# Four pieces per low half on GpSimd, rank preparations one step earlier, and the second weights fetched from SyncE

## The chip, the cores and the metric

The kernel runs on one core of a Trainium2 chip. The time is that of the whole program on the device in microseconds; three executions are given by their median. In this text PE is TensorE, DVE is VectorE, ACT is ScalarE, POOL is GpSimd and SP is SyncE, which here only issues DMAs.

## The reference, cut to what matters

Three layers follow each other. Attention over 4 batches, 8 heads, 576 positions and a head size of 64, with a window of 32 in heads 0 to 3 and a dilated window in heads 4 to 7. Then a mixture of 8 experts in which each of the 2304 tokens goes to the one expert with the largest gate value. Then a dense layer with a rational activation.

```python
logits = x @ w_gate + modality_bias[modality_id]        # x: [2304, 512] from the attention
e_idx = np.argmax(logits, axis=1)
for e in range(8):
    mask = e_idx == e
    h = np.maximum(x[mask] @ w1[e], 0.0)                # w1[e]: [512, 1024]
    out[mask] = gate_w[mask, None] * (h @ w2[e])        # w2[e]: [1024, 512]
# then: h = x @ w_in; g = P(h) / (Q(h) + 1e-6); g @ w_out
```

## The kernel before, in words

Every product is done in float32 by halves: a float32 matrix is split into a high half (an ACT copy to the matmul's number format) and a low half (the rest, one subtraction), and three matmuls, high by high, high by low and low by high, are summed in PSUM.

The attention is a pipeline of 36 steps, `for g in range(NG)`. In each step PE makes the scores of four blocks (`step_s`, line 485), DVE adds the mask and finds the maximum (line 489), ACT takes exponentials (`step_e`, line 496), PE transposes them (`step_t`, line 503), DVE copies the transposes (line 505), PE multiplies by the values (`step_v`, line 515) and DVE divides (lines 520 to 529). PE also transposes q and k for later steps (`qk_T`, lines 463 and 469) and works through `tasks`, a list of the gate's transposes and matmuls (lines 549, 562, 567). Engines run their instructions in the order in which the program writes them, so the order in a step is the order on each engine.

The first half of the tokens (`bp` 0) is finished in the middle of this loop. From then on `soon`, a list built by `ahead`, adds one small piece of work to each step: counting, choosing the expert with the most tokens (`choose`), fetching its first weights (`fetch`), building one-hot rows (`spread`, line 318), then `take`, which finds that expert's first 256 tokens and gathers them through two indirect DMAs of POOL (line 365), then `order` (lines 371 to 379), which prepares ranks for the other experts, and at last a reduction of what `order` left on POOL (line 303). `take` runs at the end of step 33, `order` at the end of step 34, the reduction at the end of step 35.

When the last q and k are transposed, at the end of step 33, their load buffers are given up (`lctx.close()`), and the split first weights (`w1s`) and the raw second weights (`raw2`) get that memory. In steps 34 and 35 and right after the loop ACT and POOL split the first expert's first weights, `raw1`, in eight chunks of 128 x 512: ACT copies the high half (line 130), POOL subtracts the low half (line 131). After the loop ACT reads the chosen expert's number, and it issues the two 1 MB loads of `raw2` (`fetch2`, line 213).

After the loop PE ends the attention while it starts the first slot of 128 tokens of the chosen expert: `stage_1` (lines 146, 148, 150) with the first weights, then the second half of the gate (lines 562 to 579, `pick` on DVE, lines 283 to 289), the ranks of the second half (lines 850, 851, 295, 297), a chain of small DVE instructions that ends in the table of token places (lines 865 to 892), and PE's product with that table (line 907). Between these, PE does the slot's second matmuls (`mm2_first`: lines 803 and 805 for chunks 0 to 7, then line 809). ACT and POOL split the second weights in eight chunks meanwhile (`hi2`, line 784; `lo2`, line 788). The four matmuls of chunks 0 and 1 and the four of chunks 2 and 3 stand ahead of line 907 on PE, those of chunks 4 to 7 behind it. The first pieces of `stage_1` for the second slot stand ahead of line 907 too.

The remaining slots follow, with weights swapped where the expert changes, and then the dense layer.

SP issues nearly all DMAs in program order. `put_x` writes finished attention rows to DRAM: 20 DMAs for the third quarter (lines 602 and 605, written at step 29), two for the last (line 593, written after the loop).

Of the kernel before, what the change touches and what calls it, by code (L numbers as in the profile page):

```python
# [85 lines left out]
PL = 1  # L86
NSLOT = 25
NC2 = NSLOT + 8
TINY = 32
# [39 lines left out]
def split(nc, src, hi, lo, kk, eng):  # L129
    nc.scalar.activation(out=hi[:, kk], in_=src[:, kk], func=AF.Copy)  # L130
    eng.tensor_tensor(out=lo[:, kk], in0=src[:, kk], in1=hi[:, kk].bitcast(F32), op=ALU.subtract)


# [33 lines left out]
def fused(ctx, tc, io):  # L167
# [155 lines left out]
    def ahead(ps):  # L323
# [46 lines left out]
        def order():  # L370
            low = C("lower").rearrange("p (a b) -> p a b", a=8)
            V.tensor_scalar(out=nfo, in0=fo, scalar1=-1.0, scalar2=1.0, op0=ALU.mult, op1=ALU.add)
            V.scalar_tensor_tensor(out=nfe[:, 0, :], in0=C("slot")[:, 0:8], scalar=1.0, in1=nfo[:, 0, :], op0=ALU.add, op1=ALU.mult)
            V.tensor_scalar(out=o16, in0=nfe, scalar1=KEY, scalar2=None, op0=ALU.mult)
            V.tensor_tensor(out=LB, in0=low, in1=fo.to_broadcast([128, 8, 8]), op=ALU.max)
            nc.gpsimd.tensor_tensor(out=LB, in0=LB, in1=nfo.rearrange("p o e -> p e o").to_broadcast([128, 8, 8]), op=ALU.mult)
            V.scalar_tensor_tensor(out=c16[:, 0, :], in0=fo[:, 0, :], scalar=256.0, in1=c0, op0=ALU.mult, op1=ALU.max)
            V.scalar_tensor_tensor(out=R0[:, 0:HT], in0=nfe.to_broadcast(N9), scalar=KEY, in1=R0[:, 0:HT], op0=ALU.mult, op1=ALU.add)
            own.append(own_rank(R0, 0, nc.gpsimd))

        return [[], [count], [choose, fetch, place], [place2], *[[lambda i=i, j=j: spread(i, j)] for i in range(2) for j in range(2)], [take], [order], [lambda: own.pop()()]]

    with ExitStack() as actx, tc.manual_schedule(), nc.allow_low_precision(reason="integers"):
# [249 lines left out]
        nsp = 0  # L633
        done_V = 2
        for g in range(NG):
            if g < NG:
# [18 lines left out]
            if w1s:  # L655
                for _ in range(2):
                    if nsp < 8:
                        n, kk = divmod(nsp, 4)
                        split(nc, raw1[n], w1s[0][n], w1s[1][n], kk, nc.gpsimd)
                        nsp += 1  # L660
            if 0 <= g - LAG1 < NG - 1:
# [11 lines left out]
            if done_T == 4 * NU and not w1s:  # L673
# [3 lines left out]
                wr2 = w2ctx.enter_context(tc.tile_pool(name="wraw2", bufs=1, side="right", reuse_waits="tile"))  # L677
                raw2.extend(wr2.tile([128, 4, 512], F32, name=f"raw2{n}") for n in range(2))
            if done_L < NC and done_T >= 8 * (done_L - 1):
                load(done_L)  # L680
                done_L += 1
# [4 lines left out]

        def split1(n):
            nonlocal nsp
            for i in range(nsp, nsp + n):
                split(nc, raw1[i // 4], w1s[0][i // 4], w1s[1][i // 4], i % 4, nc.gpsimd)  # L690
            nsp += n

        e = nc.scalar.value_load(ft[0:1, 0:1], min_val=0, max_val=7)
        for n in range(2):
            fetch2(n, e, nc.scalar)
        step_e(NG - 1)
# [30 lines left out]
def moe(ctx, tc, io, sh):  # L727
# [57 lines left out]

    def lo2(c, eng):
        n, kk = divmod(c, 4)
        eng.tensor_tensor(out=w2l[n][:, kk], in0=raw2[n][:, kk], in1=w2h[n][:, kk].bitcast(F32), op=ALU.subtract)

# [40 lines left out]
    sh["spread"](0, 0)  # L830
    lo2(0, nc.gpsimd)
    fill(slot0, 2)
    tasks.pop(0)()
    for c in range(1, 8):
        if c == HC:
            fill(slot0, F1)
        hi2(c)
        lo2(c, nc.vector if c in () else nc.gpsimd)
    sh["spread"](0, 1)
# [792 lines left out]
```

## Time and profile before

| what | value |
|---|---|
| median of three executions | 826.1 us (820.74 to 828.68) |
| profiled execution, its own time | 826.8 us |
| its span, first to last instruction | 825.0 us |
| granted TensorE clock, mean | 0.979 |
| PE busy | 791.3 us, 96% of the span |
| DVE busy | 577.6 us |
| ACT busy | 509.7 us |
| POOL busy | 149.0 us |
| chain that ended last | PE 83%, DMA 8%, DVE 4%, ACT 3% |

Times inside the profile count from the first instruction. The own time of the profiled execution is 1.8 us longer than its span. A granted clock of 1.00 is the higher level of TensorE's clock (2.4 GHz), 0.50 the lower (1.2 GHz). The chain is found by going back from the last instruction, at each step to what released it.

### The profile page before, as it was taken

To read this page: it belongs to the slowest core of one execution; us is meant where nothing else is said; L and a number is where in the kernel's file an instruction comes from. 1 tells how busy PE (TensorE), PEld (TensorE's weight loads), DVE (VectorE), ACT (ScalarE), POOL (GpSimd) and SP (SyncE) were. 2 spreads that over 40 slices of the span, in tenths; PEclk is the share of its full clock that TensorE was granted. 3 is DMA by queue.
4 is the path that set the end of the run, shared out by engine and by line. 5 is a ranking of instruction groups with operands and counts; after the bars stand their busy time and mean duration, and the time that the engine had idled before them with its cause. 6 is when DMAs were issued, how large, how long until landed. Compare 5 with 4: busy or idle time off the path is not lost.

```text
span 825.0 us, 15207 instructions
## 1 busy us (share of the span) xinstructions
PE 791.3 (96%) x5277; PEld 638.4 (77%) x5279; DVE 577.6 (70%) x1370; ACT 509.7 (62%) x993; POOL 149.0 (18%) x191
## 2 busy tenths in 40 slices
PE   7899997899998999999989999999999999999995
PEld 4777765687786678888768888888888888999894
DVE  3776788932252224895599987887788888888894
ACT  4655666234253325663689878777687678778783
POOL 2011008421110101231174512000020002001001
PEclk9998899999999999999999999999999999999998
DMA  7968947195947686774011001200020001001001
GB/s 189 160 145 150 191 147 199 51 339 211 333 153 288 247 306 209 236 276 158 18 39 39 14 1 38 66 1 1 0 69 22 1 0 65 1 1 38 1 1 38
DMA packets 73509, 91.58 MB, mean 111 GB/s; under 512 B 33577, under 2 KB 43323, under 8 KB 73403
## 3 DMA queue, kind: packets, MB, share of 16 engines
q1 hardware_dynamic: 68531, 76.38, 32.7%
q0 software_dynamic: 3360, 11.03, 3.8%
q10 hardware_dynamic: 1512, 2.91, 1.1%
q8 instruction: 48, 0.79, 0.4%
q14 instruction: 58, 0.48, 0.2%
HBM read 75.59 MB, written 14.71 MB: 109 GB/s over the span
## 4 chain that ended last, share of the span: by engine, by line
PE 83%; DMA 8%; DVE 4%; ACT 3%; issue 1%; SPq 0%; POOL 0%; POOLq 0%; ACTq 0%; DVEq 0%
PE p1t L1363 8%; PE p1t L1364 8%; PE p1t L1365 8%; DMA sw<-in_w 5%; PE p1t L146 4%; PE p1t L150 4%; PE p1t L148 4%; PE pht L1533 4%; PE pht L1534 3%; PE pht L1535 3%; PE pot L777 3%; PE pot L775 3%; PE pot L779 3%; PE pot L1535 2%; PE pxt L1533 2%; PE pxt L1534 2%
## 5 line engine op out<-in xcount | busy, mean ns | idle before, releaser
L1481 ACT ACTIVATE raw<-p1t 128x512 f32<-128x512 f32 (+1 forms) x78 | 43.2, 554 | 81.9 <-PE p1t L1365 77.0
L1488 DVE TENSOR_TENSOR raw<-raw,raw 128x512 f32<-128x512 f32 (+1 forms) x80 | 52.0, 649 | 59.0 <-ACT raw L1482 58.2
L768 DVE TENSOR_TENSOR hl<-pht,hh 128x512 fp32r<-128x512 f32 x34 | 21.9, 685 | 97.9 <-ACT hh L767 92.7
L1365 PE MATMUL p1t<-yh,wl 128*128 128x512 f32 (+1 forms) x240 | 89.0, 371 | 0.0
L1544 POOL DMA_INDIRECT out<-hs,row x10 | 10.9, 1087 | 302.2 <-ACT hs L1542 300.8
L1482 ACT ACTIVATE raw<-raw,bab 128x512 f32<-128x512 f32 (+1 forms) x80 | 61.9, 773 | 2.7
L1363 PE MATMUL p1t<-yh,wh 128*128 128x512 f32 (+1 forms) x160 | 59.6, 372 | 0.3 <-DVE m L1499 0.3
L1364 PE MATMUL p1t<-yl,wh 128*128 128x512 f32 (+1 forms) x160 | 59.2, 370 | 0.0
L1510 DVE SCALAR_TENSOR_TENSOR m<-m,nab,raw 128x512 f32<-128x512 f32 (+1 forms) x80 | 58.6, 733 | 0.1
L146 PE MATMUL p1t<-w1h,xh 128*128 128x512 f32 x144 | 57.7, 401 | 0.1
L150 PE MATMUL p1t<-w1h,xl 128*128 128x512 f32 x144 | 56.7, 393 | 0.0
L148 PE MATMUL p1t<-w1l,xh 128*128 128x512 f32 x144 | 56.4, 392 | 0.0
L1508 DVE SCALAR_TENSOR_TENSOR raw<-raw,raw 128x512 f32<-128x512 f32 (+1 forms) x80 | 56.4, 705 | 0.0
L1483 ACT ACTIVATE raw<-p1t,nab 128x512 f32<-128x512 f32 (+1 forms) x78 | 56.1, 719 | 0.0
L1490 ACT ACTIVATE raw<-raw,bab 128x512 f32<-128x512 f32 (+1 forms) x80 | 53.7, 671 | 0.5 <-DVE raw L1488 0.4
L1499 DVE SCALAR_TENSOR_TENSOR m<-m,nab,p1t 128x512 f32<-128x512 f32 (+1 forms) x78 | 53.5, 685 | 0.1
L775 PE MATMUL pot<-w2h,hh 128*128 128x512 f32 x128 | 52.0, 406 | 0.0
L777 PE MATMUL pot<-w2l,hh 128*128 128x512 f32 x128 | 51.6, 403 | 0.0
L1506 DVE SCALAR_TENSOR_TENSOR raw<-raw,raw 128x512 f32<-128x512 f32 (+1 forms) x80 | 51.6, 645 | 0.0
L1497 DVE TENSOR_TENSOR m<-raw,p1t 128x512 f32<-128x512 f32 (+1 forms) x78 | 49.3, 632 | 2.7
L779 PE MATMUL pot<-w2h,hl 128*128 128x512 f32 x128 | 50.6, 395 | 0.0
L489 DVE CUSTOM_DVE_ANT_0 pe<-sc,mask 128x96 f32<-128x96 f32 x144 | 28.4, 253 | 31.6 <-PE sc L485 19.6
(374 smaller groups left out, 2110.5 us busy)
## 6 DMA issues: line engine op xcount, KB each, us to landing
sw<-in_w SPq DMA_DIRECT2D x80, 256.0 KB
raw<-in_w SPq DMA_DIRECT2D x10, 1024.0 KB
dr<-in_w_in SPq DMA_DIRECT2D x16, 512.0 KB
dr<-in_w_out SPq DMA_DIRECT2D x16, 512.0 KB
y<-ys_rows SPq DMA_DIRECT2D x18, 256.5 KB
ldq<-in_q SPq DMA_DIRECT2D x16, 288.0 KB
ys_rows<-yo SPq DMA_DIRECT2D x17, 256.5 KB
ldk<-in_k SPq DMA_DIRECT2D x14, 288.0 KB
```

Source lines behind the costliest of these rows:

```text
L146: nc.tensor.matmul(out=p, lhsT=xh[:, kk], rhs=wh[n][:, kk], start=(kk == 0), stop=False)
L148: nc.tensor.matmul(out=p, lhsT=xh[:, kk], rhs=wl[n][:, kk], start=False, stop=False)
L150: nc.tensor.matmul(out=p, lhsT=xl[:, kk], rhs=wh[n][:, kk], start=False, stop=(kk == 3))
L775: nc.tensor.matmul(out=p, lhsT=a[:, c], rhs=w2h[n][:, kk], start=(c == 0), stop=False)
L777: nc.tensor.matmul(out=p, lhsT=a[:, c], rhs=w2l[n][:, kk], start=False, stop=False)
L779: nc.tensor.matmul(out=p, lhsT=b[:, c], rhs=w2h[n][:, kk], start=False, stop=(c == 7))
L1363: nc.tensor.matmul(out=p[:, 0:n], lhsT=wh(kk)[:, cs], rhs=ab[0][:, kk, 0:n], start=(kk == 0), stop=False)
L1364: nc.tensor.matmul(out=p[:, 0:n], lhsT=wh(kk)[:, cs], rhs=ab[1][:, kk, 0:n], start=False, stop=False)
L1365: nc.tensor.matmul(out=p[:, 0:n], lhsT=wl(kk)[:, cs], rhs=ab[0][:, kk, 0:n], start=False, stop=(kk == 3))
L1482: nc.scalar.activation(out=v, in_=ah, func=AF.Identity, scale=bab[:, 1:2], bias=bab[:, 0:1])
L1508: nc.vector.scalar_tensor_tensor(out=v, in0=v, scalar=2.0, in1=r, op0=ALU.subtract, op1=ALU.mult)
L1510: nc.vector.scalar_tensor_tensor(out=m, in0=m, scalar=nab[:, 0:1], in1=v, op0=ALU.add, op1=ALU.mult)
```

## The change: what it does

Three edits. A new function `low_part` does the subtraction for one 128 x 512 chunk as four POOL instructions of 128 columns (`PW`), for the eight chunks of the first weights and the eight of the second weights of the first expert; later swaps still use `split`. The first three DVE instructions of `order` go to the end of the step before, behind `take`; the other five, two of which are on POOL, stay in their step as `order2`. The loads of `raw2` are issued by SP at the end of step 33, where the memory changes hands, and no longer by ACT after the loop.

```diff
+PW = 128
+def low_part(nc, src, hi, lo, kk):
+    for c in range(0, 512, PW):
+        cs = slice(c, c + PW)
+        nc.gpsimd.tensor_tensor(out=lo[:, kk, cs], in0=src[:, kk, cs], in1=hi[:, kk, cs].bitcast(F32), op=ALU.subtract)
...
         def order():
-            low = C("lower").rearrange("p (a b) -> p a b", a=8)
             V.tensor_scalar(out=nfo, in0=fo, scalar1=-1.0, scalar2=1.0, op0=ALU.mult, op1=ALU.add)
             V.scalar_tensor_tensor(out=nfe[:, 0, :], in0=C("slot")[:, 0:8], scalar=1.0, in1=nfo[:, 0, :], op0=ALU.add, op1=ALU.mult)
             V.tensor_scalar(out=o16, in0=nfe, scalar1=KEY, scalar2=None, op0=ALU.mult)
+
+        def order2():
+            low = C("lower").rearrange("p (a b) -> p a b", a=8)
             V.tensor_tensor(out=LB, in0=low, in1=fo.to_broadcast([128, 8, 8]), op=ALU.max)
             nc.gpsimd.tensor_tensor(out=LB, in0=LB, in1=nfo.rearrange("p o e -> p e o").to_broadcast([128, 8, 8]), op=ALU.mult)
             V.scalar_tensor_tensor(out=c16[:, 0, :], in0=fo[:, 0, :], scalar=256.0, in1=c0, op0=ALU.mult, op1=ALU.max)
             V.scalar_tensor_tensor(out=R0[:, 0:HT], in0=nfe.to_broadcast(N9), scalar=KEY, in1=R0[:, 0:HT], op0=ALU.mult, op1=ALU.add)
             own.append(own_rank(R0, 0, nc.gpsimd))
-        return [..., [take], [order], [lambda: own.pop()()]]
+        return [..., [take, order], [order2], [lambda: own.pop()()]]
...
+        def split1(n):
+            nonlocal nsp
+            for i in range(nsp, nsp + n):
+                n1, kk = divmod(i, 4)
+                nc.scalar.activation(out=w1s[0][n1][:, kk], in_=raw1[n1][:, kk], func=AF.Copy)
+                low_part(nc, raw1[n1], w1s[0][n1], w1s[1][n1], kk)
+            nsp += n
...
             if w1s:
                 for _ in range(2):
                     if nsp < 8:
-                        n, kk = divmod(nsp, 4)
-                        split(nc, raw1[n], w1s[0][n], w1s[1][n], kk, nc.gpsimd)
-                        nsp += 1
+                        split1(1)
...
                 raw2.extend(wr2.tile([128, 4, 512], F32, name=f"raw2{n}") for n in range(2))
+                e = first_expert()
+                for n in range(2):
+                    fetch2(n, e)
...
-        e = nc.scalar.value_load(ft[0:1, 0:1], min_val=0, max_val=7)
-        for n in range(2):
-            fetch2(n, e, nc.scalar)
...
-    def lo2(c, eng):
+    def lo2(c):
         n, kk = divmod(c, 4)
-        eng.tensor_tensor(out=w2l[n][:, kk], in0=raw2[n][:, kk], in1=w2h[n][:, kk].bitcast(F32), op=ALU.subtract)
+        low_part(nc, raw2[n], w2h[n], w2l[n], kk)
```

## Rows read from the trace of the kernel before

**Rows 1.** The page, part 1: busy time, share of the span, instructions.

```profile
PE 791.3 (96%) x5277; PEld 638.4 (77%) x5279; DVE 577.6 (70%) x1370; ACT 509.7 (62%) x993; POOL 149.0 (18%) x191
```

**Rows 2.** Windows: stretch, length, busy time of each engine, granted clock, DMA.

```profile
126.00:136.00 10.00, 7.26 (x89) 5.36 (x89) 8.60 (x35) 7.14 (x18) 9.32 (x10) 0.83 0.82 269
148.00:160.00 12.00, 8.83 (x49) 6.93 (x48) 11.71 (x43) 2.81 (x6) 3.06 (x4) 0.86 0.07 23
```

**Rows 3.** Waits of all engines, 120 to 160 us: total, times, longest.

```profile
PE pdt L907 <- DVE ar L892: 3.2, 2, 3.0
...
PE pv L515 <- DVE pts L505: 2.2, 1, 2.2
...
DVE lg L579 <- PE pl L577: 1.9, 1, 1.9
...
PE pyt L295 <- DVE oh L289: 1.8, 1, 1.8
```

**Rows 4.** Timeline of POOL, 118 to 165 us: start, duration, what.

```profile
126.41 2.58 POOL L131 TENSOR_TENSOR w1l<-raw,w1h 128x512 fp32r<-128x512 f32 x2
128.95 0.36 POOL L376 TENSOR_TENSOR LB<-LB,nfo 128x64 f32<-128x64 f32 x1
129.28 0.32 POOL L302 TENSOR_TENSOR ow<-R,oh 128x72 f32<-128x72 f32 x1
129.56 4.95 POOL L131 TENSOR_TENSOR w1l<-raw,w1h 128x512 fp32r<-128x512 f32 x4
...
139.52 1.28 POOL L788 TENSOR_TENSOR w2l<-raw,w2h 128x512 fp32r<-128x512 f32 x1 [1.95 <-ACT w2h L784]
140.94 8.98 POOL L788 TENSOR_TENSOR w2l<-raw,w2h 128x512 fp32r<-128x512 f32 x7
```

**Rows 5.** Timeline of DVE, 126 to 153 us.

```profile
126.61 1.13 DVE L374 TENSOR_SCALAR o<-nfe 128x8 f16<-128x8 f32 x1
...
127.79 1.23 DVE L377 SCALAR_TENSOR_TENSOR c<-fo,R 128x8 f16<-128x8 f32 x1
...
142.36 1.21 DVE L286 SCALAR_TENSOR_TENSOR sc<-lg,cst 128x72 f32<-128x72 f32 x1
...
150.56 0.16 DVE L873 SCALAR_TENSOR_TENSOR ce<-nfe,st 128x8 f32<-128x8 f32 x1
...
150.87 0.36 DVE L875 SCALAR_TENSOR_TENSOR gk<-cst,st 128x200 f32<-128x200 f32 x1
...
152.61 0.46 DVE L891 TENSOR_TENSOR am<-key,tk 128x297 f16<-128x297 f32 x1
```

**Rows 6.** One line's instructions (318): min/median/max ns, first and last start.

```profile
L318 DVE TENSOR_TENSOR bm<-hs,r x6: 479/482/1570, 110.0 to 144.7; 128x640 f16<-128x640 f16 x6
L318 DVE TENSOR_TENSOR bm<-yo,r x4: 315/316/317, 150.6 to 152.4; 128x320 f16<-128x320 f16 x4
```

**Rows 7.** The chain that ended last, end of the stretch: start, length, what.

```profile
154.52 0.66 PE pdt L907 x9
...
158.55 1.84 PE pot L809 x8
```

**Rows 8.** Timeline of PE and DVE around the moved preparations.

```profile
120.58 0.46 PE L469 MATMUL pq<-ident,ldk 64*128 64x64 f32 x4
...
123.46 0.26 DVE L489 CUSTOM_DVE_ANT_0 pe<-sc,mask 128x96 f32<-128x96 f32 x1 [0.47 <-PE sc L485]
...
131.30 0.22 DVE L303 TENSOR_REDUCE rt<-ow 128x9 f32<-128x72 f32 x1
```

**Rows 9.** Timeline of SP, 60 to 165 us.

```profile
116.28 21.28 SPq L605 DMA_DIRECT2D x_rows<-xu  x8
```

**Rows 10.** Waits of SP's queue, 85 to 165 us: total, times, longest.

```profile
SPq L605 <- DMA raw<-in_w: 20.4, 2, 16.5
```

**Rows 11.** One line's instructions (213), ACT's queue.

```profile
L213 ACTq DMA_DIRECT2D raw<-in_w x2: 389/403/417, 127.0 to 127.6; - x2
```

**Rows 12.** Groups of POOL's instructions by line and shape, whole span.

```profile
L1416 POOL TENSOR_TENSOR wl<-w,wh 128x512 fp32r<-128x512 f32 x20 | 30.4, 1522 | 26.4 <-ACT wh L1405 25.7
```

More of the change, by code (lines that the diff above doesn't have):

```diff
@@ L379, in order @@
             own.append(own_rank(R0, 0, nc.gpsimd))
-        return [[], [count], [choose, fetch, place], [place2], *[[lambda i=i, j=j: spread(i, j)] for i in range(2) for j in range(2)], [take], [order], [lambda: own.pop()()]]
+        return [[], [count], [choose, fetch, place], [place2], *[[lambda i=i, j=j: spread(i, j)] for i in range(2) for j in range(2)], [take, order], [order2], [lambda: own.pop()()]]
     with ExitStack() as actx, tc.manual_schedule(), nc.allow_low_precision(reason="integers"):
@@ L685, in fused @@
                 done_V += 1
[L687 to L691, printed above, removed]
-        e = nc.scalar.value_load(ft[0:1, 0:1], min_val=0, max_val=7)
-        for n in range(2):
-            fetch2(n, e, nc.scalar)
         step_e(NG - 1)
@@ L830, in moe @@
     sh["spread"](0, 0)
-    lo2(0, nc.gpsimd)
+    lo2(0)
     fill(slot0, 2)
@@ L837, in moe @@
         hi2(c)
-        lo2(c, nc.vector if c in () else nc.gpsimd)
+        lo2(c)
     sh["spread"](0, 1)
```

## The prediction

> **What bounds the kernel now.** I read the page first: PE is busy for 96% of the span [rows 1], so a change away from PE can only win where PE stands still or runs at its lower clock. Then the windows around the three edits. From 126 to 136 us PE is busy 7.26 of 10 us at a mean granted clock of 0.83, from 148 to 160 us 8.83 of 12 us at 0.86 [rows 2]. Then PE's waits in that stretch: three matter, 2.2 us on DVE's copy of the transposes, 1.8 us on DVE's one-hot rows, 3.2 us on DVE's table [rows 3], together 7.2 us. The clock fell after two of them: 10 x 0.17 + 12 x 0.14 = 3.4 us of full-clock work more. So all that these edits could win here is 7.2 + 3.4 = 10.6 us. All three waits end on DVE, so the timeline of DVE comes next, beside that of POOL. POOL subtracts low halves at about 1.28 us each, from 126.41 and again from 139.52 to 149.92 [rows 4]. In those times DVE instructions of 8 to 72 columns last 1.13 to 1.23 us [rows 5], while one of 8 columns at 150.56, with POOL idle, lasts 0.16 [rows 5]; a 640-column one-hot instruction takes 0.48 and once, beside POOL, 1.57 [rows 6]. Line 374 starts inside the first POOL instruction of the pair from 126.41 and ends at 127.74, where that one ends (126.41 + 2.58 / 2 = 127.70); line 377 ends at 129.02, where the second ends (128.99). So a DVE instruction that reads only SBUF stands until the POOL instruction under way is over. The reduction at 131.30 reads one operand and takes 0.22 us with POOL busy [rows 8]: not every DVE instruction stands.
>
> After this stretch the last link of it in the chain is PE's eight matmuls of line 809, 158.55 to 160.39 [rows 7]. The rest of the kernel runs on PE behind them, so I count a shift of 160.39 one to one on the end.
>
> The Trainium skill (SBUF — State Buffer, section SBUF: two separate sides) says of this pair of engines that whichever starts first holds the shared ports for its whole instruction and the other is fully blocked; the trace agrees with the half in which DVE is blocked (1.13 to 1.23 us).
>
> **Pieces of 128 columns: what a piece costs.** No 128-column subtraction stands in the trace. Nearest rows on POOL: 64 columns 0.36, 72 columns 0.32, 512 columns 1.28 [rows 4]. The line through 72 and 512 gives (1.28 - 0.32) / 440 = 2.2 ns a column and 0.44 us for 128; through 64 and 512 it gives 0.49. Started back to back they overlap a little: from 128.95 to 129.28 to 129.56 the starts lie 0.33 and 0.28 apart, and four large ones take 4.95, so 1.22 from start to start; the line through 0.28 and 1.22 gives 0.40. I take 0.42 from start to start, between 0.40 and 0.44. Lower bound 0.36 (the 64-column one, as if columns were free), upper bound 0.52: the same subtraction at 512 columns takes 1.52 beside a busy DVE [rows 12], 1.19 times 1.28, and 0.44 x 1.19 = 0.52. A chunk goes from 1.28 to 4 x 0.42 = 1.68; 16 chunks make 64 pieces, 26.9 us against 20.4.
>
> A rule that speaks against this edit is in the Trainium skill (GPSIMD Engine Reference, Performance versus the Vector engine): each POOL instruction pays a software dispatch, and a two-input one about 2.6 cycles a column at 1.2 GHz, 4497 ns for 2048 columns. An estimate from that page is 0.06 + 0.28 = 0.34 us a piece, and the sum would be 5 us of POOL time shorter than mine; the rows, at 0.40 to 0.49, decide.
>
> **What it wins: DVE.** *Around 126 us.* Line 374 is moved away, lines 375, 377 and 378 wait for at most one piece each: about 0.4 instead of line 377's 1.23. Line 489 of the last step starts near 127.5 instead of just behind line 377's end at 129.02 and line 378. But the reduction (131.30 before) needs POOL's line 302, which is queued behind the eight pieces of chunks 0 and 1: 126.4 + 8 x 0.42 + 0.36 + 0.32 = 130.5. So DVE waits there, and this is a new wait: everything behind it on DVE, the copy of the last transposes among it, comes only 0.8 us earlier, not 1.6. The 2.2 us wait of PE [rows 3] falls to some 0.6, and the clock should stay up here (1.7 us of work at stake). What is late next is that copy, then ACT's copies of chunks 6 and 7, which stand ahead of the first slot's transposed rows: I count the start of the first slot 1.5 us earlier.
>
> *136 to 141 us.* POOL paused 1.95 us before line 788 began at 139.52 [rows 4]. That pause is used up, since the first weights' low halves now end at about 126.4 + 0.7 + 32 x 0.42 = 140.5. Seven DVE instructions that ran free there now wait up to a piece each, 2 to 2.5 us in all; DVE waited 1.9 us for PE ahead of the gate's last logits [rows 3], so this eats the cover and costs about 0.3.
>
> *141 to 155 us.* Before, three small instructions and a 640-column one around the ranks, and three behind them, stood for about one POOL instruction each (1.21 and 1.57 are two of them [rows 5, 6]), some 8 us for seven. With pieces a standing one takes about 0.45, the 640-column one 0.8. Line 286 began at 142.36 [rows 5]; 1.5 earlier from the start, 0.3 later again and some 0.45 won on the one ahead of it make 140.7, and itself, a reduction, line 289 and the ranks' matmuls (0.45, 0.25, 0.45, 0.4) bring the ranks to 142.2. So the 1.8 us wait on the one-hot rows nearly goes. Behind the ranks there is less to win: POOL is now busy until about 156, and some 17 more DVE instructions (lines 310 to 892), free before (0.16 to 0.46 [rows 5]), each lose up to 0.4. 20 instructions by 0.42, with 2 us for the long ones (320 columns 0.32 x4, 200 columns 0.36 x2, 297 columns 0.46 x4 [rows 5, 6], less what fits into POOL's own gaps), are 10.4 us from 142.2: the table is done near 152.6, where line 907's last nine matmuls began at 154.52 [rows 7], and they end near 153.3.
>
> **What it costs: POOL's last chunk.** POOL is now without a pause from 126.4: 0.6 for lines 376 and 302, 26.9 for the pieces and 2.1 for long DVE instructions that make it wait: 156.0. Before, it was done at 149.92 and nobody waited. Chunks 0 to 3 end at 140.5 + 1.68 each, 147.3, about 1 us after PE wants the last, but that stall lies inside PE's wait for the table. Chunk 7 is the binding one: line 805 of chunk 7 can't end before 156.0 + 0.25, then line 809's 1.84: 158.1 against 160.39. From DVE alone it would be 153.3 + eight matmuls at the lower clock (3.4) + 1.84 = 158.5. The two lie 0.4 us apart, so the likely sum is a gain of 2.0 to 2.3 us; I take 2.3. Bounds: pieces of 0.36 end POOL at 152.2, and DVE's chain sets the end, 4 to 5 us won; pieces of 0.52 end it at 162.4, line 809 ends at 164.5, 4.1 us lost.
>
> **Preparations moved up.** Three DVE instructions (0.16, 0.17 and, free, about 0.16) go to 123.0, behind the index of `take`. DVE waited 0.47 us for PE there [rows 8]; the three take about 0.5, so they cost nothing to 0.1. POOL does nothing but DMA gathers then, and none of the three issues anything. If the cover fails, line 489 of step 34 starts 0.5 us later, which is a bound, and PE has work queued for longer. The gain is inside the sum above: line 374's 1.13 us.
>
> **Second weights from SP.** Removed from ACT: a value load and two issues of 0.40 [rows 11], beside exponentials that did not wait for them: 0. SP reads the expert's number and issues the loads at the end of step 33, after line 469's last transposes at 120.58 [rows 8], but queued behind the 20 stores of `put_x`. SP stood 16.5 us in those stores until a raw weight landed [rows 10], so that eight of them took from 116.28 to 137.56 [rows 9]; one issue of 0.6 fits ahead of the wait, so it ended near 116.9 + 16.5 = 133.4, and the raw weight that landed then can only be ACT's load of 127.0 [rows 11]. That load now stands behind the stores and can't hold them. The seven issues behind the wait took 133.4 to 137.56, 0.6 each; from 116.9 on they and one more end at 121.7, so the loads go out near 121.8 instead of 127.0. They were not waited for before (line 784 followed the program's order), so 5 us earlier buys nothing; SP's last stores come some 16 us earlier and nobody waited for them. What it may cost: the loads now share the DMA engines with POOL's two gathers, issued ahead of 126.41; the first slot's rows are needed after 130. Bounds 0 to 1 us; I take 0, as a load's first half took 6.4 us (127.0 to 133.4) beside the same gathers, and from 121.8 that is 128.2.
>
> **The rivals.** *All the standing goes.* 10.6 us: 816.2 in the profiled execution, 815.5 against the median. For it: three waits with one cause. Against it: POOL's 26.9 us must fit in before chunk 7 is used.
> *POOL becomes the bound.* If DVE's instructions hold POOL off for their full length, POOL loses not 2.1 but about 6 us (0.48 + 4 x 0.32 + 2 x 0.36 + 4 x 0.46 + 11 x 0.16 from [rows 5, 6]); it ends at 159.9, line 809 at 162.0: 1.6 us slower, 827.7. With pieces of 0.49 and 2.1 of holds it is 2.5 slower, 828.6. It decides when POOL's mean from start to start, holds included, passes (158.3 - 127.0) / 64 = 0.49; I have 0.45. For it: there is no slack left. Against it: seven POOL instructions with DVE's seven between them took 8.98, 1.28 each, as the one at 139.52 [rows 4]. The rule of the shared ports above, in the Trainium skill (SBUF — State Buffer, section SBUF: two separate sides), is this case: a DVE instruction that starts first blocks POOL as well.
> *The pieces change nothing.* As many more DVE instructions stand as each stands shorter; the table comes at 154.5 again: 826.
> *The loads come late.* If SP's stores still stand until 139, the loads go out 12 us later than ACT's; a first half lands 6.4 us after its issue, near 145.4, and line 784, which ran just ahead of 139.52 [rows 4], waits: 7 us slower, 833.
>
> **How the numbers follow.** Forecast: 826.8 - 2.3 = 824.5 for the profiled execution, which is 0.7 above the median of 826.1; so 823.8. Chances: forecast 0.45, all goes 0.07, POOL bound 0.23, nothing changes 0.20, loads late 0.05. The bounds alone reach from 5 won (821.1) to 4.1 lost (830.2), and the executions before lie up to 5.4 below and 2.6 above their median; a median of few can lie half of that off. For 8 in 10 I take 818.0 to 829.5, which leaves out the first and the last rival and the far tails. About 1% is what can be told from no change here, 8.3 us: below 817.8 there is the first rival and a little of the forecast's tail, 0.08; above 834.4 a part of the late loads and of POOL at its worst, 0.05; the rest, 0.87, within.
>
> **What would show it.** In the profile after: 64 POOL pieces of 0.40 to 0.45; lines 377, 284, 286, 867, 869 and 307 at 0.3 to 0.6; lines 310 to 892 longer than before while POOL is busy; line 303 waiting on POOL; POOL without a pause from 126 to about 156 and a wait of PE's line 805 on line 788; SP's stores of `put_x` done by 122 and the loads out just behind them. I am wrong if a piece costs over 0.5, if the DVE chain sets the end alone, or if a wait further on takes the gain back.

## The result, and the profile after

The changed kernel takes 829.99 us (median of 20; 824.35 to 840.02) against 826.97 us for the kernel before beside it (median of 20), 3.0 us more. The ratio is 1.0068, 95% interval 1.0042 to 1.0094: 5.6 us slower (3.5 to 7.8). It leaves out executions more than 1.5% above the fastest of their kernel, and as the profiled executions of two experiments (second weights whole, and overlapping pieces of 256) were such ones, only durations on DVE and POOL are read from these two. The forecast was 823.8 us, a gain of 2.3 us. The profiled execution after took 827.59 us, its span 825.8 us, against 826.8 and 825.0 before. In what follows, line numbers are those of the changed kernel, up to 10 higher than before (307 is now 314, 805 is 815, 809 is 819); the subtraction is line 138.

I measure the stretch that the edits touch from the end of the last transposes of q and k (the mark, in what follows) to the end of the eight matmuls of line 809 (now 819). Before, it lasted 160.39 - 121.04 = 39.35 us [rows 7, 8]. After, the timeline of PE (start, duration, what) gives 164.17 - 120.59 = 43.6 us, 4.2 more:

```profile
120.13 0.46 PE L478 MATMUL pq<-ident,ldk 64*128 64x64 f32 x4
...
140.49 0.21 PE L860 MATMUL pyt<-c,ident 128*128 128x80 f16 x1
...
151.56 0.23 PE L302 MATMUL pyt<-oh,upper 128*128 128x80 bf16 x1 [10.82 <-DVE oh L296]
...
159.17 1.22 PE L917 MATMUL pdt<-ar,bm 128*128 128x33 f16 x18
...
162.18 1.99 PE L819 MATMUL pot<-w2h,hl 128*128 128x512 f32 x8
```

PE came to the ranks' first matmuls 2.3 us earlier than before (line 860 at 140.49; 142.80 before), 1.9 us of it counted from the mark, then stood 10.82 us for the one-hot rows. The waits of all engines from 120 to 165 us (total, times, longest) show that this one took the place of the three in [rows 3]:

```profile
PE pyt L302 <- DVE oh L296: 10.8, 1, 10.8
...
DVE rt L310 <- POOL ow L309: 1.2, 1, 1.2
...
PE px L143 <- DVE pts L514: 1.0, 1, 1.0
```

The wait for the transposes fell from 2.2 to 1.0 us, the one for the table is gone, and the new wait of the reduction on POOL is there as forecast. The windows that answer to [rows 2] show a gain up to 136 us (PE 8.76 us busy where it was 7.26, clock 1.00 where it was 0.83), and then the loss:

```profile
126.00:136.00 10.00, 8.76 (x103) 6.10 (x104) 8.07 (x33) 7.41 (x19) 10.00 (x25) 1.00 0.50 184
136.00:148.00 12.00, 4.73 (x25) 2.69 (x25) 11.90 (x5) 5.61 (x11) 12.00 (x30) 0.90 0.43 93
148.00:160.00 12.00, 8.44 (x53) 6.87 (x53) 10.36 (x36) 3.74 (x6) 5.74 (x13) 0.67 0.01 1
```

In the second of them DVE is "busy" for 11.90 of 12 us with five instructions. Its timeline says which; the first three are the moved preparations:

```profile
122.45 0.16 DVE L378 TENSOR_SCALAR nfo<-fo 128x8 f32<-128x8 f32 x1
122.64 0.17 DVE L379 SCALAR_TENSOR_TENSOR nfe<-cst,nfo 128x8 f32<-128x8 f32 x1
122.84 0.17 DVE L380 TENSOR_SCALAR o<-nfe 128x8 f16<-128x8 f32 x1
...
134.89 11.72 DVE L314 CAST rb<-rt 128x9 int32<-128x9 f32 x1
146.65 0.37 DVE L317 TENSOR_SCALAR tk<-rb 128x9 int32<-128x9 int32 x1
147.05 0.37 DVE L318 TENSOR_SCALAR rb<-rb 128x9 int32<-128x9 int32 x1
147.46 0.78 DVE L320 TENSOR_SCALAR r<-rb 128x9 f16<-128x9 int32 x2
...
150.97 0.53 DVE L296 TENSOR_TENSOR oh<-sc,mx 128x72 bf16<-128x72 f32 x1
```

A cast of 9 columns stood for 11.72 us. In the kernel before, it took 0.41:

```profile
137.19 0.41 DVE L307 CAST rb<-rt 128x9 int32<-128x9 f32 x1
```

The cast lay beside POOL's run, which has no pause from 125.95 on (the rows that answer to [rows 4]):

```profile
125.95 3.42 POOL L138 TENSOR_TENSOR w1l<-raw,w1h 128x128 fp32r<-128x128 f32 x8
129.33 0.29 POOL L385 TENSOR_TENSOR LB<-LB,nfo 128x64 f32<-128x64 f32 x1
129.58 0.32 POOL L309 TENSOR_TENSOR ow<-R,oh 128x72 f32<-128x72 f32 x1
129.86 10.03 POOL L138 TENSOR_TENSOR w1l<-raw,w1h 128x128 fp32r<-128x128 f32 x24
139.84 13.89 POOL L138 TENSOR_TENSOR w2l<-raw,w2h 128x128 fp32r<-128x128 f32 x32
```

Some 28 pieces passed while the cast stood. From 146.61 on most DVE instructions of this kind waited for about one piece (0.36 to 0.53), as forecast, though POOL ran on without a pause until 153.73. SP's timeline and its queue's waits answer to [rows 9] and [rows 10]: the stores of `put_x` are out by 121.05, the loads follow at 121.87, and the wait of 16.5 us is 2.4.

```profile
116.08 4.31 SPq L614 DMA_DIRECT2D x_rows<-xu  x8
120.44 0.61 SPq L611 DMA_DIRECT2D x_rows<-xu  x1
121.87 1.07 SPq L220 DMA_DIRECT2D raw<-in_w  x2
```

```profile
SPq L614 <- DMA raw<-in_w: 3.2, 2, 2.4
```

In the profiled pair PE is 3.8 us late at line 819 and 0.8 us at the end. The rest is taken back from 245 to 275 us, where PE waits for loads of weights anyway. The windows of before, then of after: idle 2.09 us at a clock of 0.89 before, 1.33 at 1.00 after.

```profile
245.00:260.00 15.00, 12.91 (x131) 9.15 (x129) 0.69 (x1) 2.45 (x5) 1.32 (x3) 0.89 0.99 348
```

```profile
245.00:260.00 15.00, 13.67 (x96) 9.63 (x98) 4.13 (x8) 3.67 (x8) 3.46 (x5) 1.00 0.94 333
```

The ratio shows more than that pair, 5.6 us; which of its executions a profile catches matters, since those of the kernel before lie between 816.07 and 833.53.

### The profile page after: what moved, and what is told of

It is laid out like the page before. It is cut to its first block, busy times and chain, and to the rows that moved or that the text cites. A ratio compares the mean times of both kernels' runs of the same rounds, so it can differ in the third digit from the quotient of the medians.

```text
span 825.8 us, 15248 instructions
## 1 busy us (share of the span) xinstructions
PE 790.9 (96%) x5279; PEld 638.5 (77%) x5279; DVE 582.1 (70%) x1370; ACT 509.1 (62%) x993; POOL 156.5 (19%) x239
## 4 chain that ended last, share of the span: by engine, by line
PE 47%; ACT 2%; DVE 1%; POOL 0%; issue 0%; POOLq 0%; ACTq 0%
PE p1t L1373 7%; PE p1t L1374 7%; PE p1t L1375 7%; PE pht L1543 4%; PE pht L1544 4%; PE pht L1545 3%; PE pot L1545 2%; PE pxt L1543 2%; PE pxt L1544 2%; PE pxt L1545 2%; PE pot L1544 2%; PE pot L1543 2%; DVE raw L1498 0%; ACT raw L1492 0%; PE pdt L1358 0%; PE pyt L1358 0%
## 5 line engine op out<-in xcount | busy, mean ns | idle before, releaser
L1375 PEld LDWEIGHTS p1t<-yh,wl 128*128 128x128 f32 x240 | 45.0, 188 | 6.3
```

Source lines behind the costliest of these rows:

```text
L1375: nc.tensor.matmul(out=p[:, 0:n], lhsT=wl(kk)[:, cs], rhs=ab[0][:, kk, 0:n], start=False, stop=(kk == 3))
```

## The experiments

The question was why one cast stood for 28 pieces. The theories: (A) the size of POOL's instruction decides, small ones let no turn; (B) there is a turn behind every instruction, as I had predicted, and the cast stood for something else; (C) the loads or the moved preparations cost the time, not the pieces; (D) a stand is a fixed time of some 12 us; (E) POOL's instructions that follow each other without a gap keep DVE out until the run breaks. All runs of the whole kernel in one table: the stretch as measured above and the first cast of line 314, in us and each from one execution, and the ratio with its interval.

```
kernel                                 stretch  cast   ratio (95%)
before                                  39.4    0.41   1
after                                   43.6   11.72   1.0068 (1.0042 to 1.0094)
e1  whole chunks, other edits kept      38.0    1.31   1.0016 (0.9979 to 1.0053)
e2  pieces alone                        45.1   11.75   1.0064 (1.0026 to 1.0101)
e3  two pieces of 256                   43.4   13.63   0.9989 (0.9953 to 1.0024)
e4  one wait of POOL between weights    39.0    3.78   1.0038 (1.0003 to 1.0074)
e5  first weights whole                 37.2    0.97   1.0009 (0.9976 to 1.0041)
e9  the same again                      35.4    1.37   0.9991 (0.9951 to 1.0030)
e6  second weights whole                  -    13.61   1.0072 (1.0024 to 1.0119)
e7  every piece waits for the last      45.5    0.47   1.0127 (1.0077 to 1.0178)
e8  the same, pieces of 256               -     0.63   1.0005 (0.9969 to 1.0041)
e10 one wait in 8 pieces                41.2    0.48   1.0058 (1.0025 to 1.0090)
e11 one wait in 4 pieces                42.0    0.38   1.0093 (1.0060 to 1.0126)
```

**Which edit.** `e1_whole`: `PW = 512`, all else as changed.

```diff
-PW = 128
+PW = 512
```

> The changed kernel with whole chunks of 512 columns instead of four pieces; the moved preparations and the loads from SyncE stay. Theory A: no long stand of VectorE's first cast after the loop, which ends about 0.5 us after it starts; line 809's counterpart ends about 2 us earlier than in the kernel before (158.4 against 160.39), ratio to the kernel before 0.995 to 1.000. Theory C (the early loads or the moved preparations cost the time, not the pieces): as slow as the changed kernel, ratio 1.005 or more.

`e2_pieces_only`: the kernel before with `low_part` for both weights, no moved preparations, loads from ACT.

```diff
-                        split(nc, raw1[n], w1s[0][n], w1s[1][n], kk, nc.gpsimd)
+                        nc.scalar.activation(out=w1s[0][n][:, kk], in_=raw1[n][:, kk], func=AF.Copy)
+                        low_part(nc, raw1[n], w1s[0][n], w1s[1][n], kk)
...
-        eng.tensor_tensor(out=w2l[n][:, kk], in0=raw2[n][:, kk], in1=w2h[n][:, kk].bitcast(F32), op=ALU.subtract)
+        low_part(nc, raw2[n], w2h[n], w2l[n], kk)
```

> The kernel before with the pieces of 128 columns alone. Theory A: a stand of several us of the first cast after the loop, as in the changed kernel, and a ratio of 1.003 to 1.012. Theory B: no stand above 0.8 us; ratio 0.996 to 1.003. Theory C: as the kernel before.

Without pieces nothing stands over 1.6 us and no loss can be told; with pieces alone the ratio is that of the full change, and the cast stands as long. (C) falls. The two also say where the gain up to 136 us comes from. The first slot's transposes (line 143) start 11.2 us behind the mark in the kernel before, 10.2 with pieces alone, 9.3 with the other edits alone and 10.2 with all three: each brings something by itself, and in these executions, one of each kernel, the pieces add nothing to what the moved preparations bring.

**What ends the stand.** `e4_pool_waits`: the changed kernel with one tiny copy on POOL between the last piece of the first weights and the first of the second; it reads `tk`, which DVE writes behind the cast, so POOL pauses there.

```diff
+    nc.gpsimd.tensor_copy(out=sh["hole2"], in_=sh["tk"][:, 0:1])
```

> The changed kernel with one tiny copy on GpSimd between the first and the second weights' pieces, which reads what VectorE writes right after the cast, so that GpSimd stops there until the cast is through. Theory A: the cast ends near 140.3 instead of 146.6, where the first weights' pieces end; some later stands may come; the last second matmuls end 3 to 6 us earlier than in the changed kernel; ratio to the kernel before 0.995 to 1.003. Theory B: GpSimd only loses the wait, no gain: ratio as the changed kernel, 1.005 to 1.010.

The timelines of DVE and of POOL:

```profile
134.25 3.78 DVE L315 CAST rb<-rt 128x9 int32<-128x9 f32 x1
138.07 0.17 DVE L318 TENSOR_SCALAR tk<-rb 128x9 int32<-128x9 int32 x1
138.28 0.18 DVE L319 TENSOR_SCALAR rb<-rb 128x9 int32<-128x9 int32 x1
```

```profile
128.01 9.99 POOL L138 TENSOR_TENSOR w1l<-raw,w1h 128x128 fp32r<-128x128 f32 x24
138.31 0.19 POOL L842 COPY hole<-tk 128x1 int32<-128x1 int32 x1 [0.31 <-DVE tk L318]
```

POOL's run ends at 138.00, the cast at 138.03. So the stand isn't a fixed time, and (D) falls: it ends with the run. `e3_pw256` (`PW = 256`), `e5_first_whole` and `e6_second_whole` (one of the two weights in whole chunks again, by an argument of `low_part`) ask for the size:

```diff
-def low_part(nc, src, hi, lo, kk):
-    for c in range(0, 512, PW):
-        cs = slice(c, c + PW)
+def low_part(nc, src, hi, lo, kk, w=PW):
+    for c in range(0, 512, w):
+        cs = slice(c, c + w)
...
-                low_part(nc, raw1[n1], w1s[0][n1], w1s[1][n1], kk)
+                low_part(nc, raw1[n1], w1s[0][n1], w1s[1][n1], kk, 512)
```

> The changed kernel with two pieces of 256 columns a chunk. Theory A: if what matters is that an instruction follows the last without a gap, whatever its length, a stand as with 128 columns; if length matters, 256 columns lie between: waits of up to 0.7 us each and no stand, ratio 0.997 to 1.003. Theory B: 0.7 us a wait, no stand.

> The changed kernel with whole chunks for the first weights and pieces of 128 columns for the second. Theory A: the first cast after the loop waits for one whole chunk (about 1.3 us) and gets in; among the second weights' pieces a stand of several us can come at a later instruction of VectorE that has to wait, up to 12 us. Theory B': only the run already under way when the cast arrives matters, and from then on each instruction waits for one piece (0.4 to 0.5): no stand above 1.4 us, and the last second matmuls near 159. Ratio to the kernel before 0.997 to 1.004 without a stand, 1.005 to 1.010 with one.

> The changed kernel with pieces of 128 columns for the first weights and whole chunks for the second. Theory A: the first cast after the loop stands from about 135 to the end of the pieces, near 140, 5 us, and gets in at the first boundary beside a whole chunk (up to 141.5); later ones wait up to 1.3 us each. Theory D (a stand lasts about 12 us, whatever GpSimd runs): it ends at 146.6 as in the changed kernel. Ratio to the kernel before 1.000 to 1.006 under A, 1.006 or more under D.

In e3 the cast stood from 132.19 to POOL's end at 145.8, although pieces of 256 are twice as long. In e6 it was asked for during the pieces and then got no turn between eight whole chunks either (DVE, then POOL):

```profile
145.92 13.61 DVE L314 CAST rb<-rt 128x9 int32<-128x9 f32 x1
```

```profile
149.62 9.87 POOL L138 TENSOR_TENSOR w2l<-raw,w2h 128x512 fp32r<-128x512 f32 x8
```

POOL's end is 159.49, the cast's 159.53. (A) falls: whole chunks keep DVE out as well, once it is out. In e5 the cast came when nine POOL instructions had started since the last pause, and it got its turn; from then on every DVE instruction got one in the 32 pieces too:

```profile
133.57 0.97 DVE L314 CAST rb<-rt 128x9 int32<-128x9 f32 x1
```

`e9_first_whole_again` repeats e5:

> Whole chunks for the first weights and pieces for the second once more, now in five rounds, since three left the sign open: in its profile the second matmuls ended some 3 us earlier than in the kernel before, counted from a mark ahead of the three edits. If that reaches the end: ratio 0.994 to 0.999. If what follows takes it back: 0.999 to 1.003.

Both ratios hold 1: no gain that can be measured, though the stretch was 2 to 4 us shorter in both profiles.

**What lets it begin.** Four kernels of their own have POOL subtract without end while DVE asks for casts of 9 columns. In `m1_lock` all pieces write the same columns, so each waits for the one before, 79 ns of gap.

```python
for _ in range(int(STREAM / (0.126 + 0.00217 * w))):
    nc.gpsimd.tensor_tensor(out=lo[:, 0:w], in0=src[:, 0:w], in1=hi[:, 0:w].bitcast(F32), op=ALU.subtract)
```

> A kernel that computes nothing of the reference: twelve stretches in which GpSimd subtracts without a pause for about 12 us, in instructions of 512, 256, 128, 64, 192 or 96 columns, while VectorE runs some one-operand reductions and then six casts of 9 columns (or six subtractions of 72 columns). Theory A (in a run of short GpSimd instructions the next takes the shared port before the last lets go, so VectorE gets no turn): at 512 columns the first cast takes about 1.2 us or less, at 128 and 64 columns it stands for several us, up to the end of the run. Theory B (one GpSimd instruction per turn, whatever its length): casts of 1.2, 0.65, 0.4 and 0.28 us at 512, 256, 128 and 64 columns, none above 0.8.

Nothing stood: six casts took 1.59 us beside pieces of 128, 2.41 beside 256. That agreed with (B), and misled me until the gaps were seen. `m2_runs` gives each piece columns of its own, so that they overlap in the records by 40 ns and more, as in the changed kernel (36 to 63):

```diff
+            o = i * w
-            nc.gpsimd.tensor_tensor(out=lo[:, 0:w], in0=src[:, 0:w], in1=hi[:, 0:w].bitcast(F32), op=ALU.subtract)
+            nc.gpsimd.tensor_tensor(out=lo[:, o:o + w], in0=src[:, 0:w], in1=hi[:, 0:w].bitcast(F32), op=ALU.subtract)
```

> As the first kernel by itself, which computes nothing of the reference, but each GpSimd subtraction writes columns of its own, so that none waits for the one before: in the first kernel by itself they stood 79 ns apart, in the changed kernel each began some 40 ns before the end of the last. Eleven runs of 16.5 or 33 us, of 64 to 512 columns. Theory A (without a gap between them VectorE gets no turn among short instructions): with 128 columns the first cast stands for the rest of the run or about 12 us; with 512 columns about 1.2 us. Theory B (one turn per instruction also without a gap): 0.4 to 0.5 us a cast at 128 columns, as behind 146.6 us in the changed kernel.

Now five of eleven sections stood: 11.44 to 16.29 us at 128, 12.75 at 192, 12.76 at 512; others, at 128 and 512 too, took one turn for each instruction. What set them apart was how long POOL had run since its last pause or DVE's last turn. `m3_when` puts a real pause ahead of each section and asks early and late (`at` is in us):

```diff
+        nc.vector.tensor_reduce(out=end, in_=lo[:, o:o + 8].bitcast(F32), op=ALU.add, axis=AX.X)
...
-        for _ in range(pre):
+        for _ in range(int(at / 0.264)):
             one_input()
```

> By itself, nothing of the reference: fourteen runs of GpSimd subtractions without a gap, each begun after a pause of GpSimd, and three casts of VectorE that come 3 to 17 us into the run, which goes on for some 26 us; widths 128, 256 and 512. The last run is of 128 columns with each instruction writing what the one before wrote, so that it waits for it. Theory E (a run without a gap puts GpSimd's cores out of step, and from some point on VectorE gets no turn): casts 3 and 5 us into the run wait for one instruction, casts from about 9 us on stand for 10 us or more; the point is reached later with fewer, longer instructions; in the last run none stands. Theory A (short instructions alone): 128 columns stand at every time, 512 at none.

The casts on DVE's timeline, three to a row, for 128 columns asked at 4.8, 6.9, 9.0, 10.8 and 13.9 us behind the start of the run:

```profile
43.10 1.11 DVE L55 CAST i<-f 128x9 int32<-128x9 f32 x3
...
77.06 12.32 DVE L55 CAST i<-f 128x9 int32<-128x9 f32 x3
...
113.10 10.22 DVE L55 CAST i<-f 128x9 int32<-128x9 f32 x3
...
150.95 8.39 DVE L55 CAST i<-f 128x9 int32<-128x9 f32 x3
...
192.18 5.24 DVE L55 CAST i<-f 128x9 int32<-128x9 f32 x3
```

The four that stood all came in 18.36 us behind the start of their run, at the 45th piece, while POOL went on. At 256 columns one asked at 12.9 us stood 26.05 us to the run's end, at 512 none stood up to 16.8 us. By time the sizes differ; by number of instructions they might agree. `m4_count` asks around that number, and adds runs in which every 8th or 16th piece waits for the one before:

```diff
+            b = 1 if every and i and i % every == 0 else 0
+            nc.gpsimd.tensor_tensor(out=lo[:, o - b:o + w], in0=src[:, 0:w + b], in1=hi[:, 0:w + b].bitcast(F32), op=ALU.subtract)
```

> A kernel of its own that computes nothing of the reference, one look. Each section begins with a real pause of POOL, then one size of subtraction follows itself on columns of its own, and three casts of 9 columns are asked for late in the run, at a chosen number of POOL instructions behind the pause: 128 columns at 14, 15 and 16; 256 at 15, 16 and 17; 512 at 15, 16, 17 and 20; 64 at 15, 17, 20, 26, 31 and 46. The run goes on some 12 us after that. In five last sections (128 columns, asked at 22, 27 and 35) every 8th or every 16th piece also writes the last column of the piece before and so has to wait for it. In the kernel before this one casts stood 7.6 to 26 us when 17 or more instructions of 128, or 19 of 256, had run since the pause, and at most 0.9 us for 14 or fewer of any size. Theory of a count: from 15 to 17 instructions on the first cast stands for over 5 us at 128, 256 and 512 columns alike, and with a break every 8 none stands over 0.9. Theory of a time or an overlap that adds up: the bound differs between the sizes, 512 stands at none of 15 to 20 if it goes by us (at 17 us none stood), and 64 stands late or never. Rival, that a break does nothing: the sections with breaks stand like 128 columns without, 4 to 12 us.

```
columns   started since the pause: the first cast stood, us (* to the run's end)
64        15: 3.12   17: 2.60   20: 2.09   25: 0.23   30: 0.28   44: 0.16
128       14: 0.29   15: 11.69*  16: 11.84*   (m3: 12: 0.28, 17: 11.51, 22: 9.41)
256       15: 11.18*  16: 11.33*  17: 11.22*  (m3: 14: 0.67, 19: 26.05*)
512       15: 0.81   16: 10.45*  17: 10.61*  20: 10.60*   (m3: 14: 0.35)
128, a wait in 8:   22: 0.42   26: 0.16   33: 0.20
```

Each entry is one cast in one execution, and the tiny copy on POOL that opens each section isn't counted. The runs of this kernel end about 12 us behind the request, so a star is no duration of its own. With a wait in 16 the casts came at the 11th and the 2nd piece behind a wait and took 0.26 and 0.36, which says nothing of the bound. Rows of it (128 at 14 and 15, 512 at 15 and 16, 128 with a wait in 8 at 33):

```profile
14.14 1.12 DVE L56 CAST i<-f 128x9 int32<-128x9 f32 x3
...
32.37 12.11 DVE L56 CAST i<-f 128x9 int32<-128x9 f32 x3
...
148.78 3.25 DVE L56 CAST i<-f 128x9 int32<-128x9 f32 x3
...
178.64 10.86 DVE L56 CAST i<-f 128x9 int32<-128x9 f32 x3
...
431.57 1.02 DVE L56 CAST i<-f 128x9 int32<-128x9 f32 x3
```

In these runs the count decides, not the time: up to 14 instructions since the pause (or since DVE's last turn) a turn, from 16 on none, for 128, 256 and 512 alike, 6 us of run at 128 and 19 us at 512. A wait in 8 keeps the count low, and nothing stands. That is (E), with a number. In the changed kernel 23 POOL instructions had started since the pause when the cast came, in e2, e4 and e6 26, in e3 only 15; the kernel before never has more than 9 in a row, 8 in this stretch. Each pause here is made by a wait, so whether the gap or the wait gives DVE its turn isn't told apart.

**A gap at every piece.** `e7_overlap` lets each piece also write the last column of the one before, so that it waits; `e8_overlap256` is the same with pieces of 256.

```diff
-        cs = slice(c, c + PW)
+        cs = slice(max(c - 1, 0), c + PW)
```

> The changed kernel in which each piece but a chunk's first begins one column earlier, on the last column of the piece before, which it writes again with the same value, so that it waits for that piece. Theory E: no stand above 0.6 us; the cast ends near 135.4; GpSimd's 64 pieces take some 5 us more, so the last low half comes near 159 and sets the end of the second matmuls, near 161; ratio to the kernel before 0.998 to 1.005. If waits for one piece were not what lets VectorE in: a stand of 10 us as before, ratio 1.006 to 1.012.

> The same with two pieces of 256 columns a chunk, so one such wait a chunk. Theory E: no stand above 1 us (a stand of 13.6 us with 256 columns and no waits); GpSimd ends near 155; last second matmuls 1 to 2 us earlier than in the kernel before; ratio 0.994 to 1.001. Otherwise a stand as without the waits, ratio 0.995 to 1.003 as measured there.

Nothing stands, and in e7 the ranks come 8.7 us sooner behind the mark than in the changed kernel. Still e7 is the slowest of all, well over the 0.998 to 1.005 that I expected: POOL takes 35.4 us for its pieces, and PE waits 7.1 us for `w2l`.

**A gap now and then.** `e10_break8` overlaps once in two chunks, `e11_break4` once in each (without the test of `kk`).

```diff
-        cs = slice(c, c + PW)
+        cs = slice(c - 1 if c == PW and kk % 2 == 0 else c, c + PW)
```

> The changed kernel, with the second piece of every other chunk also writing the last column of the first, so that POOL waits for its own instruction once in 8 pieces (0.12 us each, 8 of them, 1.0 us of POOL time in all); the result of that column is written twice with the same value. If only POOL's runs without a gap keep DVE out, the cast of line 314 waits for at most the pieces up to the next break, below 3.4 us, and more likely for one piece, 0.4 to 0.5; the table is then done some 4 to 8 us earlier than in the changed kernel, and the time is between 821 and 825, ratio 0.995 to 1.000. If breaks do nothing, the cast stands 11 to 12 us and the ratio is 1.005 to 1.008. If the breaks cost more than they free, as the overlap of every piece did, over 1.003 without a stand.

> The same with the wait once in every chunk, 4 pieces (16 waits, 1.9 us of POOL time in all). No stand over one piece by the theory of runs without a gap; POOL ends 1 us later than with one wait in 8, so if POOL's last chunk sets the end the time is 0.5 to 1 us longer than that run, and the same if DVE does. If breaks do nothing, the cast stands 11 to 12 us.

The stand is gone in both, and both are slower than the kernel before still (for e10 I had expected 0.995 to 1.000). In e10 the cast takes 0.48 us, and POOL and PE show the new bound:

```profile
131.06 0.48 DVE L314 CAST rb<-rt 128x9 int32<-128x9 f32 x1
```

```profile
125.83 10.69 POOL L138 TENSOR_TENSOR w1l<-raw,w1h 128x128 fp32r<-128x128 f32 x24
136.48 16.99 POOL L138 TENSOR_TENSOR w2l<-raw,w2h 128x128 fp32r<-128x128 f32 x32
```

```profile
144.25 0.51 PE L815 MATMUL pot<-w2l,hh 128*128 128x512 f32 x1 [0.78 <-POOL w2l L138]
...
150.54 0.80 PE L815 MATMUL pot<-w2l,hh 128*128 128x512 f32 x1 [0.60 <-POOL w2l L138]
...
153.52 0.80 PE L815 MATMUL pot<-w2l,hh 128*128 128x512 f32 x1 [1.76 <-POOL w2l L138]
154.12 3.61 PE L819 MATMUL pot<-w2h,hl 128*128 128x512 f32 x8
```

```profile
150.00:160.00 10.00, 7.70 (x19) 5.66 (x20) 9.69 (x38) 0.00 (x0) 6.88 (x10) 0.55 0.30 94
```

PE waits for chunk 7 until POOL ends at 153.47, and its clock has gone to 0.55, so line 819 takes 3.61 us for 1.84 [rows 7]. With 128-column pieces and the first limit removed, the stretch ends 1.9 us later than in the kernel before, by POOL's end.

## Why the prediction was wrong, point by point

**The step that failed** is the sentence that a DVE instruction reading only SBUF stands until the POOL instruction under way is over, and with it "wait for at most one piece each". It was read from [rows 4] and [rows 5], where it is true: there POOL never has more than 8 instructions in a row, and up to 14 the kernels by themselves show a turn behind each. The change made a run of 66, and the first DVE instruction of the standing kind that came late in it stood 11.72 us in place of 0.4. I had written that POOL would have no pause from 126 to 156 and priced that as a lost cover of 0.3 us; it was what the forecast turned on: the ranks' matmuls, forecast to be done at 142.2, began at 151.56. One sign of being wrong that I had named, that the DVE chain sets the end alone, came true. The Trainium skill (SBUF — State Buffer, section SBUF: two separate sides) has the lock end with the instruction that holds it; beside the short runs of the kernel before the trace agrees (1.13 to 1.23 us for instructions of 1.28), in a long run it does not (11.72 us for pieces of 0.45).

**The rival that came true behind it** is POOL as the bound, priced at 1.6 us slower (its second price, 2.5 with pieces of 0.49, comes to 2.2 by its own terms). With the stand removed (e10) the stretch is 1.9 us longer than before and the ratio 1.0058. Two terms were short. POOL lost to DVE's turns 31.1 us (64 pieces in e10) - 26.9 - 1.0 (eight waits) = 3.2 us, not 2.1; 26.9 is the forecast's time for the pieces, and with the measured 0.41 a piece it is 3.9. And behind POOL's end I counted 0.25 + 1.84 = 2.1 us at the full clock; it took 4.3, since PE's waits brought the lower clock. PE's waits for `w2l`, a sign that I had named, are absent in the changed kernel and come in e10 (3.1 us in three). So with pieces of 128 columns no cure of the stand brought the forecast gain.

**Right:** a piece costs 0.41 us from start to start (forecast 0.42); POOL ended at 153.73 (forecast 156.0), 0.45 us of it by an earlier start and most of the rest by turns that DVE didn't take. The moved preparations took 0.16 to 0.17 each at 122.45 and cost nothing. The first slot's transposes (line 143) start at 130.81 where they started at 132.22, 1.4 us earlier (forecast 1.5); that it fits so well is in part luck, since 0.45 of it lies ahead of the edits and counted from the mark the gain is 1.0, as with the pieces alone (e2), and less than the 1.9 without them (e1). The new wait on line 309 came (1.2 us). The loads go out at 121.87 (forecast 121.8) and cost nothing that can be told: e1, with both of these edits, is the same as before within its interval, which reaches to 1.0053.

**The rivals that fell:** not all standing went (816); the loads were not late (833); "the pieces change nothing" fell as a sum, though e3 and e8 come out there.

**What stays open.** Why the run has to be 15 or 16 long; why a stand at 128 columns ends by itself (18.4 us behind the run's start in m3, 20.7 to 22 in the changed kernel, e2 and m2, 7.1 at 64 columns) and at 256 and 512 only with the run; and e3, where the cast stood although only 13 instructions had started since DVE's last turn, 15 since the pause. The ratio doesn't follow the stretch in each row (e3 is no slower with 4.0 us more in it, e4 is slower with 0.4 less): each stretch is one execution, each ratio is known to some 3 to 4 us, and how much of the 5.6 us lies outside the stretch isn't settled. Nor is its size: over all 20 executions the medians lie only 3.0 us apart.

By the ratios alone a plainer rule fits better than the stand. Each kernel with 128-column pieces for the first weights is slower than the one before (1.0038 to 1.0127), and each other holds 1 (0.9989 to 1.0016), e3 with its stand of 13.63 us among them. So the runs show that these pieces cost the time, and the trace shows the stand make the stretch longer; that the stand, and not POOL's longer work, makes up the 5.6 us isn't shown. Part of the noise has a place: in the eleven profiles other than e6 and e8 the mark lies between 116.5 and 128.6 us, and no edit has begun there. From the mark to the end of the span the kernel before takes 704.0 us, the changed one 705.2 and e3 705.5, one execution each.

No version beat the kernel before: e1, e3, e5 with e9, and e8 stand within 0.2% of it, with intervals that hold 1.

## What to carry to other kernels

A rule read from a trace (one wait per instruction) holds for the spacing that the trace has; a change that closes the pauses must be tried against the longest run that it makes, not the mean. Where GpSimd and VectorE share a stretch, keep GpSimd's runs below 15 instructions (up to 14 DVE got its turn here), or let one of them wait for its own predecessor (0.12 us here), and ask what four times as many instructions cost the engine that pays for them. Cure one limit and measure again before trusting its price: here, with the stand gone, a second limit kept the stretch 1.9 us longer than before the change.

## What the runs showed of the hardware

- Beside a run of GpSimd subtractions without a gap, a VectorE instruction that stands beside GpSimd at all (a cast of 9 columns here) gets its turn within one of them if at most 14 have started since the pause or its last turn, and from 16 on stands 4 to 26 us, by how late it comes and when the run ends (128, 256 and 512 columns alike; at 64 columns 2 to 3 us for one that comes at 15 to 20, and at 25 and later a turn again). At 128 columns turns come again behind the 45th to 55th instruction even in a run without a gap. One cast, that of e3, stood at 15 since the pause and 13 since DVE's last turn.
- A GpSimd instruction that waits for its own predecessor starts 79 ns behind it (m1); without that wait it starts 43 ns before the other's end in m3, 36 to 63 in the changed kernel. That 0.12 us, once in 8 pieces, is all the difference between a cast of 0.48 us (e10) and one of 11.72.
- The Trainium skill (GPSIMD Engine Reference, section Instruction dispatch) says that GpSimd's cores go on to the next instruction each as it is done with its share. The overlap of 43 ns agrees; that it is the cause of the stand is not shown, since the same overlap is there in the first 14 instructions, and e2's cast stood for 11.75 us beside one of 36.
